# A gated MLP on one core: another order of products seven, three and four, and of the raw products, in the pairs of pass one

## Chip, cores and metric

The kernel runs on one core of a Trainium2 chip. The metric is the device time of one execution in microseconds (us); the median of three runs is compared. In the text TensorE is PE, its weight loads PEld, VectorE DVE, ScalarE ACT, GpSimd POOL, and SP is the engine whose queue issues all the DMAs here.

## What is computed

A gated feed-forward layer on 2048 rows, with inputs and weights in bf16 (x 2048 x 1024, the hidden size is 3584):

```python
g = jnp.einsum("bsd,df->bsf", x, w_gate)
u = jnp.einsum("bsd,df->bsf", x, w_up)
h = _gelu(g) * u
return jnp.einsum("bsf,fd->bsd", h, w_down)
```

## The kernel before

**Passes and units.** The 2048 rows are done in two passes of two blocks of 512 rows. In a pass, the first half makes h: 14 units, each with 256 columns of w_gate and 256 of w_up. The second half multiplies by w_down.

**Products.** A unit treats gate and up as 2 x 2 blocks and multiplies them with seven block products instead of eight. Sums of weight blocks (`s1` to `s4`, made by POOL, and `sa`, a cast by ACT) meet sums of x blocks (`t1` to `t4`, `tb`); these are 128 x 512 matmuls in float32 (fp32r operands). Two of the seven products need no sums: the raw products `raw1` and `raw2` multiply w by x in bf16. A block product is four matmuls for gate and four for up, so eight in all; a half product (`part`) has four.

**Pairs.** In pass one the units 4 to 11 run as four pairs, by `pair0` (L347). Unit a = 4, 6, 8 or 10 is the first of its pair and b = a + 1 the second; n = a + 2 and nn = a + 3 are the units of the next pair, whose raw products the pair computes ahead. Within a pair, the product s1 x t1 of both units is done with half products (`r1` to `r4` and halves of `s1` against `T1` to `T4`, `TB`), whose result for unit b, and that of unit a, is also written to DRAM (`pd`) for use in pass two.

**Banks.** The eight PSUM banks are four pairs of two, called F, C, K and E in a pair; index 0 is gate, 1 is up. A matmul without a fresh start adds to what stands in the bank. So between two products in one bank, other engines copy out (`snap`, ACT), add to it in place (`add`, DVE) or read it (`gelu` on ACT, then `times` on DVE, which multiplies gelu of gate by up into h and reads up from the bank).

**Side work.** The sums of w_down that the second half needs are also made within the pairs, by `keep(j, n, ps)` in three steps: each step is a cast of a w_down piece into a PSUM bank (ACT, L517) and a subtraction (DVE, L518). The three steps use the banks ps[0], ps[1], ps[0], and step two and three subtract the result of the step before. A pair does this for `ja` at its beginning in K, for `jm` (pairs 4 and 6 only, from MID) in its middle in F, and for `jb` at its end in C. `hooks("made", j)` stores such a result, `hooks("fetch", a)` (L416) fetches the next pair's `ja`, `hooks("w", n)` loads the weights of unit n, `hooks("pd", .)` stores to `pd`; all of them are issued by SP in the order of the text.

**What sets the order.** `manual_schedule` keeps the order in which the code issues instructions on PE, DVE, POOL and SP, and within a pass on ACT too. So each engine's queue is the text of `pair0` filtered for that engine, and a product waits where its bank has not been released.

**The PE order of a pair before**, in block products with the bank that they go to:

```
F s2·t2 | E half | C s2·t2 (b) | E half | F s3·t3 | E s4·tb | K r2 half | F sa·t4 |
K r3 half | E r1 half | C s3·t3 (b) | E r4 half | K half |
F raw1 (n) | E raw2 (n) | K s4·tb (b) | C sa·t4 (b) | E raw1 (nn) | K raw2 (nn)
```

These are 124 matmuls, 92 in float32 and 32 in bf16. At the beginning of the next pair its own first half product in E is copied out (`p1`, L377) before the second half product adds to the same bank (L382); the copies stand in ACT's queue behind the gelu of the last raw product of the pair before, one cast of `keep(ja, 0, K)` and the two `u2` copies.

Of the kernel before, what the change touches and what calls it, by code (L numbers as in the profile page):

```python
# [10 lines left out]
def kernel(  # L11
# [32 lines left out]
    ADD, SUB, MUL = ALU.add, ALU.subtract, ALU.mult  # L44
# [17 lines left out]
    JS = {4: (0, 2), 6: (3, 5), 8: (6, 7), 10: (8, 9)}  # L62
    MID = {4: 1, 6: 4}
# [45 lines left out]
    def dve(out, a, b, op):  # L109
        nc.vector.tensor_tensor(out=out, in0=a, in1=b, op=op)  # L110
# [14 lines left out]
    def snap(ps, name, at=None):  # L125
        t = slot([P, N], f32, name) if at is None else at
        nc.scalar.copy(out=t, in_=ps)  # L127
        return t
# [71 lines left out]
    def gelu(src):  # L200
        g = slot([P, N], f32, "g")
        nc.scalar.activation(g, src, ACT.Gelu_apprx_tanh)  # L202
        return g
# [3 lines left out]
    def times(fb, c, g, u):  # L207
        if (fb, c) not in away:
            at = h(fb // NJ, fb % NJ, c)
        else:  # L210
            at = away[fb, c] = away[fb, c]()
        dve(at, g, u, MUL)
# [14 lines left out]
    def add(ps, other):  # L227
        g = new(dve, ps[0], other[0], ADD, "sum", dtype=f32)
        dve(ps[1], ps[1], other[1], ADD)
        return g, ps[1]  # L230
# [85 lines left out]
    def part(ps, lhs, rhs, start, stop=True):  # L316
        for i in range(2):
            for k in range(H):
                matmul(ps[i], lhs[i][:, k, :], rhs[k], start and k == 0, stop and k == H - 1)

    def full(ps, lhs, rhs, start=False):
        for i in range(2):
            product(ps[i], lhs[i], rhs, start)

    def raw1(e, w):
        full(e, [w[:, i, :KH, :P] for i in range(2)], [xT[0][:, k] for k in range(KH)], True)

    def raw2(c, w):
        full(c, [w[:, i, KH:, :P] for i in range(2)], [xT[0][:, KH + k] for k in range(KH)], True)

    def hadd(ps, other, fb, c):
        g, up = add(ps, other)
        g = gelu(g)
        times(fb, c, g, up)
# [8 lines left out]
    def squared(e, p5, fb):  # L343
        dve(e[1], e[1], p5[1], SUB)
        times(fb, 0, gelu(e[0]), e[1])

    def pair0(a, roles, S, t, js, hooks):  # L347
        F, C, K, E = roles
        b, n, nn = a + 1, a + 2, a + 3
        sa, sb = S[a], S[b]  # L350
        q = {}
        t1 = t["t1"]
        A, B = [[flat(xT[1][:, 2 * m : 2 * m + 2]) for m in (2 * n, 2 * n + 1)] for n in range(2)]

        sa.make(*[x for x in ("s1", "s2", "s3") if x not in sa])
        sb.make(*[x for x in ("s1", "s2") if x not in sb])
        form = small_sums((sa, sb), q)
        form("r1"), form("r2")
        if "s4" not in sa:
            sa.make("s4")  # L360
        form("r3")
        sb.make("s3")
        form("r4")
        sb.make("s4")

        def keep(j, n, ps):
            if j is not None:
                keep_part(j, n, ps[n % 2])

        ja, jb = js  # L370
        jm = MID.get(a)
        hooks("w", n)
        keep(ja, 0, K)
        full(F, sa["s2"], t["t2"])
        u2a = [snap(F[i], "u2") for i in range(2)]
        part(E, [x[:, :H] for x in sa["s1"]], t1[:H], True, False)
        p1 = [snap(E[i], "p1", A[i]) for i in range(2)]  # L377
        full(C, sb["s2"], t["t2"])
        keep(ja, 1, K)
        keep(ja, 2, K)  # L380
        hooks("made", ja)
        part(E, [x[:, H:] for x in sa["s1"]], t1[H:], False)  # L382
        p5a = [snap(E[i], "p5") for i in range(2)]
        u2b = [snap(C[i], "u2") for i in range(2)]
        full(F, sa["s3"], t["t3"])
        g, up = add(F, p5a)
        into(K, p1)
        full(E, sa["s4"], t["tb"])
        g = gelu(g)
        times(2 * a + 1, 1, g, up)  # L390
        part(K, q["r2"], T2, False)
        u2r = [snap(K[i], "u2", B[i]) for i in range(2)]
        full(F, sa["sa"], t["t4"])
        hadd(E, u2a, 2 * a, 1)
        part(K, q["r3"], T3, False)
        squared(F, p5a, 2 * a + 1)
        keep(jm, 0, F)
        part(E, q["r1"], T1, True)
        sb.make("sa")
        hooks("w", nn)  # L400
        p5r = [snap(E[i], "p5", A[i]) for i in range(2)]
        full(C, sb["s3"], t["t3"])
        for i in range(2):
            dve(A[i], K[i], p5r[i], ADD)
        keep(jm, 1, F)
        keep(jm, 2, F)
        part(E, q["r4"], TB, False)
        hooks("pd", b)
        part(K, [x[:, H:] for x in sb["s1"]], T4, False)
        hooks("home", b)  # L410
        for i in range(2):
            dve(B[i], E[i], u2r[i], ADD)
        hooks("pd", a)
        if jm is not None:
            hooks("made", jm)
        hooks("fetch", a)  # L416
        p5b = [snap(K[i], "p5") for i in range(2)]
        raw1(F, W(n))
        g, up = add(C, p5b)
        p1n = [snap(F[i], "p1") for i in range(2)]  # L420
        raw2(E, W(n))
        S[n], S[nn] = sums_s(W(n), pool), sums_s(W(nn), pool)
        g = gelu(g)
        times(2 * b + 1, 1, g, up)
        full(K, sb["s4"], t["tb"])
        hadd(E, p1n, 2 * n, 0)
        S[n].make("sa")
        full(C, sb["sa"], t["t4"])
        hadd(K, u2b, 2 * b, 1)
        raw1(E, W(nn))  # L430
        squared(C, p5b, 2 * b + 1)
        keep(jb, 0, C)
        p1nn = [snap(E[i], "p1") for i in range(2)]
        keep(jb, 1, C)
        keep(jb, 2, C)
        raw2(K, W(nn))
        S[n].make("s1", "s2")
        if nn <= LAST:
            S[nn].make("s1", "s2")
        hadd(K, p1nn, 2 * nn, 0)  # L440
        hooks("made", jb)
        return F, E, K, C

    def pair1(a, roles, S, t, hooks):
        F, C, K, E = roles
# [50 lines left out]
    wraw, made = {}, {}  # L496
# [119 lines left out]
    sa = {}  # L616
# [188 lines left out]
    def W(u):  # L805
        if u not in ws:
            ws[u] = load_w(u)
        return ws[u]
# [37 lines left out]
    for ip in range(NPASS):  # L846
        with tc.manual_schedule(engines={ENG.Activation}):
# [6 lines left out]
            for u in range(1 if ip == 0 else 0, NU):  # L854
                if upgraded(u):
                    if u % 2:
                        continue
                    if u == FIRST:
                        S = {u: s, u + 1: sums_s(W(u + 1), pool)}
                    if (ip, u) == (0, FIRST):  # L860
                        fetch_wd(MID.values())
                        for n in range(4):
                            for c in range(2):
                                away[NH + n, c] = lambda n=n, c=c: staged(n, c)
                        away[NH + 4, 0] = lambda: hx

                    def hooks(what, n):
                        if what == "w":
                            W(n)
                            if ip == 0 and n - 3 in JS:  # L870
                                fetch_wd(JS[n - 3][1:])
                            if ip and n <= LAST:
                                fetch_p5(n)
                        if what == "home" and n == LAST:
                            bring_home()
                        if what == "pd":
                            k = 0 if n % 2 else KH
                            nc.sync.dma_start(
                                out=pd[:, n - FIRST].rearrange("p i n -> p (i n)"),
                                in_=flat(xT[1][:, k : k + KH]),  # L880
                            )
                        if what == "made":
                            store_made(n)
                        if what == "fetch":
                            fetch_wd(JS[n + 2][:1] if n + 2 in JS else [10, 12, 13])

                    roles = F, C, K, E
                    if ip == 0:
                        F, C, K, E = pair0(u, roles, S, t, JS[u], hooks)
                    else:  # L890
                        F, C, K, E = pair1(u, roles, S, t, hooks)
                    if u + 1 == LAST:
                        s = make_s(None, pool, S[u + 2])
                        nxt["s"] = S[u + 3]
                    continue
# [19 lines left out]
                def keep(part, ps):  # L915
                    if js:
                        keep_part(js[0], part, ps[part // 2])
                    if ip == 0 and u in (2, 3):
                        for n in ((0, 1), (), (2,))[part]:
                            lo_part(u - 2, n, ps)  # L920
# [92 lines left out]
```

## Time and profile before

| what | value |
|---|---|
| median of three runs | 536.85 us (536.62 to 536.99) |
| the profiled execution, its own time | 536.99 us |
| its span, first to last instruction | 535.2 us |
| PE busy | 529.3 us |
| DVE, ACT, POOL busy | 364.9, 279.8, 261.4 us |
| granted TensorE clock | 1.000 |
| pairs of pass one begin at | 65.65, 93.28, 121.15, 149.03 us |
| unit 12 begins at | 176.90 us |

The span is the time between the first and the last instruction of the program; 1.8 us of the execution's own time lie around it. A line of the timeline gives the start of a group of equal instructions, the time from its first start to its last end, the engine, the source line, the operation with its tiles (out<-in) and shapes, the count, and in brackets the idle time before it with what ended it. Matmuls overlap: one is shown with about 0.39 us, though the next begins some 0.22 us after it, so the steps from start to start are what counts on PE. The first float32 matmul behind bf16 ones is recorded about 0.19 us early and that much longer.

### The profile page before, as it was taken

The numbers are of one execution on the slowest core, as the hardware profiler recorded it, in microseconds if no ns is written. First come the engines' busy times: TensorE is split into PE (matmuls) and PEld (weight loads), VectorE is DVE, ScalarE is ACT, GpSimd is POOL, SyncE is SP. The second block draws the span as 40 slices with busy tenths as digits, with TensorE's granted clock in tenths as the row PEclk, the third lists the DMA queues.
The fourth block names the chain that finished last, engine by engine and source line by source line (L and its number), as shares of the span: only waits on it lengthen the run. The fifth ranks groups of instructions, "written<-read, shape, count | busy, mean of one in ns | idle before, by whom it ended". The sixth has DMA issues, their size and how long they took to land.

```text
span 535.2 us, 7481 instructions
## 1 busy us (share of the span) xinstructions
PE 529.3 (99%) x2372; PEld 377.4 (71%) x2393; DVE 364.9 (68%) x568; ACT 279.8 (52%) x503; POOL 261.4 (49%) x247
## 2 busy tenths in 40 slices
PE   8999999999999999999999999999999999999997
PEld 4568686868677764688886767768667685488886
DVE  2988768787777889459695545576585749675830
ACT  2557686868586731015636555656666650105351
POOL 1179977969799610000008949693979610000000
PEclk9999999999999999999999999999999999999999
DMA  9796318685758899989987343445471149555571
GB/s 246 159 246 173 82 60 294 198 295 198 235 197 288 293 347 391 274 208 224 280 242 196 80 139 99 119 118 157 120 197 54 26 129 391 208 177 168 169 244 50
DMA packets 115527, 103.91 MB, mean 194 GB/s; under 512 B 21792, under 2 KB 97696, under 8 KB 115360
## 3 DMA queue, kind: packets, MB, share of 16 engines
q1 hardware_dynamic: 115488, 103.44, 63.9%
q8 instruction: 19, 0.31, 0.2%
q14 instruction: 20, 0.16, 0.1%
HBM read 78.64 MB, written 19.40 MB: 183 GB/s over the span
## 4 chain that ended last, share of the span: by engine, by line
PE 98%; DMA 1%; issue 0%; SPq 0%; ACT 0%
PE bank L134 98%; DMA xn<-in_x_dram 1%; SPq L705 0%; PE bank L712 0%; ACT st L677 0%
## 5 line engine op out<-in xcount | busy, mean ns | idle before, releaser
L113 POOL TENSOR_TENSOR s<-w 128x512 fp32r<-128x512 bf16 x102 | 119.8, 1195 | 152.1 <-PE bank L134 113.3
L134 PE MATMUL bank<-t,s 128*128 128x512 f32 x552 | 131.6, 392 | 0.0
L134 PEld LDWEIGHTS bank<-t,s 128*128 128x128 f32 x552 | 103.6, 188 | 22.3
L134 PE MATMUL bank<-xT,w 128*128 128x512 bf16 (+1 forms) x489 | 107.8, 376 | 1.0
L134 PEld LDWEIGHTS <-w 128*128 128x128 bf16 x504 | 47.8, 98 | 58.2 <-issue 4.4
L202 ACT ACTIVATE g<-sum 128x512 f32<-128x512 f32 x81 | 51.5, 636 | 64.6 <-DVE sum L110 64.0
L127 ACT COPY p<-bank 128x512 f32<-128x512 f32 x102 | 58.1, 590 | 50.5 <-PE bank L134 50.4
L110 DVE TENSOR_TENSOR sum<-bank,p 128x512 f32<-128x512 f32 x54 | 37.1, 687 | 39.4 <-PE bank L134 38.8
L110 DVE TENSOR_TENSOR hT<-g,bank 128x512 bf16<-128x512 f32 x72 | 49.1, 687 | 17.1 <-ACT g L202 11.3
L113 POOL TENSOR_TENSOR s<-w,s 128x512 fp32r<-128x512 bf16 x50 | 58.1, 1181 | 0.3
L113 POOL TENSOR_TENSOR s<-s,w 128x512 fp32r<-128x512 f32 x50 | 57.6, 1172 | 0.4
L122 ACT CAST tb<-raw 128x512 fp32r<-128x512 bf16 x28 | 17.5, 628 | 72.8 <-PE bank L134 31.0
L134 PE MATMUL bank<-t,sa 128*128 128x512 f32 x216 | 55.0, 397 | 0.0
L134 PE MATMUL bank<-tb,s 128*128 128x512 f32 x216 | 54.3, 393 | 0.0
L110 DVE TENSOR_TENSOR bank<-bank,p 128x512 f32<-128x512 f32 x70 | 48.5, 696 | 7.0 <-PE bank L134 6.8
L134 PE MATMUL bank<-q 128*128 128x512 f32 x208 | 51.7, 389 | 0.0
L134 PEld LDWEIGHTS bank<-t,sa 128*128 128x128 f32 x216 | 40.6, 188 | 9.1
L134 PEld LDWEIGHTS bank<-tb,s 128*128 128x128 f32 x216 | 40.5, 188 | 8.9 <-issue 0.2
L134 PEld LDWEIGHTS bank<-q 128*128 128x128 f32 x208 | 39.0, 188 | 8.1
L127 ACT COPY u<-bank 128x512 f32<-128x512 f32 x56 | 32.2, 594 | 15.1 <-PE bank L134 15.1
L110 DVE TENSOR_TENSOR q<-raw 128x512 fp32r<-128x512 bf16 x28 | 19.2, 687 | 19.2 <-DMA raw<-in_w_down_dram 16.9
L134 PE MATMUL bank<-raw,hT 128*128 128x512 bf16 x140 | 31.2, 379 | 0.2
(80 smaller groups left out, 635.2 us busy)
## 6 DMA issues: line engine op xcount, KB each, us to landing
raw<-in_w_down_dram SPq DMA_DIRECT2D x72, 256.0 KB, 5.3
w<-in_w_gate_dram SPq DMA_DIRECT2D x27, 512.0 KB, 4.3
w<-in_w_up_dram SPq DMA_DIRECT2D x27, 512.0 KB, 5.7
q<-td SPq DMA_DIRECT2D x52, 256.0 KB, 4.4
td<-m SPq DMA_DIRECT2D x12, 768.0 KB, 5.0
w<-td SPq DMA_DIRECT2D x6, 1024.0 KB, 9.6
pd<-xT SPq DMA_DIRECT2D x8, 512.0 KB, 5.9
out_dram<-st SPq DMA_DIRECT2D x32, 128.0 KB, 1.7
```

Source lines behind the costliest of these rows:

```text
L110: nc.vector.tensor_tensor(out=out, in0=a, in1=b, op=op)
L113: nc.gpsimd.tensor_tensor(out=out, in0=a, in1=b, op=op)
L122: nc.scalar.copy(out=t, in_=src)
L127: nc.scalar.copy(out=t, in_=ps)
L134: nc.tensor.matmul(ps, lhsT=lhs, rhs=rhs, start=start, stop=stop, skip_group_check=True)
L202: nc.scalar.activation(g, src, ACT.Gelu_apprx_tanh)
```

## The change

The change is in `pair0`, and in the hook that fetches `jb`. PE's order of a pair becomes:

```
F s2·t2 | E half | C s2·t2 (b) | E half | F s3·t3 | E s4·tb | K r2 half | F sa·t4 |
E r1 half | K r3 half | E r4 half | K half |
C s3·t3 (b) | K s4·tb (b) | C sa·t4 (b) |
F raw1 (n) | E raw2 (n) | C raw1 (nn) | K raw2 (nn)
```

The matmuls are the same in number and kind. `r1` goes before `r3`, the product s3 of unit b behind the half products, s4 and sa of unit b ahead of the raw products, which become one run of 32 bf16 matmuls. The `keep` of the middle moves to the product sa of unit b, in bank E, and exists in all four pairs: where MID has no entry (a = 8, 10), it takes over `jb`, and the `keep` at the end is left out. In pairs 4 and 6 the `keep` at the end stays, in E instead of C, behind the `times` of unit n. The copy of K[1] to `u2r` goes behind a gelu, the casts `sb.make("sa")` and the load of the weights of unit nn behind `gelu(F[0])`, and the fetch of the next `ja` behind the store of `jm`. The new hook fetches `jb` for pairs 8 and 10 at their beginning.

```diff
         ja, jb = js
         jm = MID.get(a)
+        if jm is None:
+            jm, jb = jb, None
         hooks("w", n)
...
         part(K, q["r2"], T2, False)
-        u2r = [snap(K[i], "u2", B[i]) for i in range(2)]
+        u2r = [snap(K[0], "u2", B[0])]
         full(F, sa["sa"], t["t4"])
-        hadd(E, u2a, 2 * a, 1)
+        g, up = add(E, u2a)
+        g = gelu(g)
+        u2r.append(snap(K[1], "u2", B[1]))
+        times(2 * a, 1, g, up)
+        dve(F[1], F[1], p5a[1], SUB)
+        part(E, q["r1"], T1, True)
+        p5r = [snap(E[i], "p5", A[i]) for i in range(2)]
         part(K, q["r3"], T3, False)
-        squared(F, p5a, 2 * a + 1)
-        keep(jm, 0, F)
-        part(E, q["r1"], T1, True)
+        for i in range(2):
+            dve(A[i], K[i], p5r[i], ADD)
+        times(2 * a + 1, 0, gelu(F[0]), F[1])
         sb.make("sa")
         hooks("w", nn)
-        p5r = [snap(E[i], "p5", A[i]) for i in range(2)]
-        full(C, sb["s3"], t["t3"])
-        for i in range(2):
-            dve(A[i], K[i], p5r[i], ADD)
-        keep(jm, 1, F)
-        keep(jm, 2, F)
         part(E, q["r4"], TB, False)
...
-        if jm is not None:
-            hooks("made", jm)
+        full(C, sb["s3"], t["t3"])
+        p5b = [snap(K[i], "p5") for i in range(2)]
+        full(K, sb["s4"], t["tb"])
+        g, up = add(C, p5b)
+        g = gelu(g)
+        times(2 * b + 1, 1, g, up)
+        full(C, sb["sa"], t["t4"])
+        keep(jm, 0, E)
+        keep(jm, 1, E)
+        dve(C[1], C[1], p5b[1], SUB)
+        keep(jm, 2, E)
+        hooks("made", jm)
         hooks("fetch", a)
-        p5b = [snap(K[i], "p5") for i in range(2)]
         raw1(F, W(n))
-        g, up = add(C, p5b)
+        g = gelu(C[0])
         p1n = [snap(F[i], "p1") for i in range(2)]
+        g2, up2 = add(K, u2b)
+        times(2 * b + 1, 0, g, C[1])
+        times(2 * b, 1, gelu(g2), up2)
         raw2(E, W(n))
         S[n], S[nn] = sums_s(W(n), pool), sums_s(W(nn), pool)
-        g = gelu(g)
-        times(2 * b + 1, 1, g, up)
-        full(K, sb["s4"], t["tb"])
-        hadd(E, p1n, 2 * n, 0)
         S[n].make("sa")
-        full(C, sb["sa"], t["t4"])
-        hadd(K, u2b, 2 * b, 1)
-        raw1(E, W(nn))
-        squared(C, p5b, 2 * b + 1)
-        keep(jb, 0, C)
-        p1nn = [snap(E[i], "p1") for i in range(2)]
-        keep(jb, 1, C)
-        keep(jb, 2, C)
+        g, up = add(E, p1n)
+        raw1(C, W(nn))
+        times(2 * n, 0, gelu(g), up)
+        keep(jb, 0, E)
+        p1nn = [snap(C[i], "p1") for i in range(2)]
+        keep(jb, 1, E)
+        keep(jb, 2, E)
         raw2(K, W(nn))
...
         hadd(K, p1nn, 2 * nn, 0)
-        hooks("made", jb)
-        return F, E, K, C
+        if jb is not None:
+            hooks("made", jb)
+        return F, C, K, E
...
-                            if ip == 0 and n - 3 in JS:
-                                fetch_wd(JS[n - 3][1:])
+                            for m in (n - 2, n - 3):
+                                if ip == 0 and m in JS and (m == n - 3) == (m in MID):
+                                    fetch_wd(JS[m][1:])
```

## Prediction

> **What bounds the kernel now.** I read the page first: the busy times and the chain of waits.
>
> ```profile
> span 535.2 us, 7481 instructions
> PE 529.3 (99%) x2372; PEld 377.4 (71%) x2393; DVE 364.9 (68%) x568; ACT 279.8 (52%) x503; POOL 261.4 (49%) x247
> ...
> PE 98%; DMA 1%; issue 0%; SPq 0%; ACT 0%
> ```
>
> PE is the bound through the whole span, and the list of waits has no entry for PE inside the four pairs. A change of order that keeps all matmuls can therefore win only what PE loses between its matmuls, and can lose without limit, by making PE wait. What it can win shows in the timeline of PE in the pair that begins at 93.28:
>
> ```profile
> 109.84 1.07 PE L134 MATMUL bank<-forms,s 128*128 128x512 f32 x4
> 110.75 3.63 PE L134 MATMUL bank<-xT,w 128*128 128x512 bf16 x15
> 114.03 2.19 PE L134 MATMUL bank<-tb,s 128*128 128x512 f32 x8
> 116.06 0.39 PE L134 MATMUL bank<-t,sa 128*128 128x512 f32 x1
> ...
> 69.28 3.11 PE L134 MATMUL bank<-t,s 128*128 128x512 f32 x13
> 124.99 3.14 PE L134 MATMUL bank<-t,s 128*128 128x512 f32 x13
> ```
>
> A float32 step is (3.11 - 0.39) / 12 = 0.227 us (row at 69.28), a bf16 step (3.63 - 0.38) / 15 = 0.217 (the run has 16, one record is missing). From 109.84 to 116.06 stand 4 + 8 float32 and 16 bf16 matmuls: 12 x 0.227 + 16 x 0.217 = 6.19, against 6.22 measured. With the first bf16 step, which is some 0.01 longer, a change to bf16 and back costs about 0.04 us.
>
> The last row shows the other thing to know. These 13 matmuls, in the pair that begins at 121.15, take 0.03 us longer than the same count in the first pair. The 23rd matmul of the pair (about 126.36) is the first that adds to E[1] again, and it needs the copy of E[1] to `p1`. Before it stand ACT and DVE:
>
> ```profile
> 119.81 0.59 ACT L127 COPY p<-bank 128x512 f32<-128x512 f32 x1 [0.28 <-PE bank L134]
> 120.30 1.11 ACT L517 CAST bank<-raw 128x512 f32<-128x512 bf16 x2
> 123.04 0.63 ACT L202 ACTIVATE g<-sum 128x512 f32<-128x512 f32 x1 [1.63 <-DVE sum L110]
> 123.58 0.58 ACT L517 CAST bank<-raw 128x512 f32<-128x512 bf16 x1
> 124.09 1.07 ACT L127 COPY u<-bank 128x512 f32<-128x512 f32 x2
> 125.05 1.09 ACT L127 COPY xT<-bank 128x512 f32<-128x512 f32 x2
> ```
>
> ```profile
> 120.92 1.49 DVE L110 TENSOR_TENSOR m<-bank,m 128x512 fp32r<-128x512 f32 x2 [0.39 <-ACT bank L517]
> 122.33 0.68 DVE L110 TENSOR_TENSOR sum<-bank,p 128x512 f32<-128x512 f32 x1
> ```
>
> The last copy (the second of the row at 125.05) ends at 126.14, 0.22 before that matmul. The three pairs with this 0.22 lose 0.03 us there, the first pair, with its copy over a microsecond earlier, nothing. So I read 0.22 us as what PE needs from the end of a release to the matmul, and the margin as used up. Everything in front hangs together: ACT is without a break from the gelu at 123.04, which waited for the sum at 122.33, which stood in DVE's queue behind the three subtractions of the `keep` at the end.
>
> **The change part by part.** Rates from these rows: ACT starts a copy every 0.48, behind a cast or gelu 0.52 to 0.54; DVE every 0.60, or 0.80 where it uses the result just before. An engine starts 0.04 after its releaser's end; a bank's last matmul counts to its shown end (start + 0.39). I put the new order on the clock of the pair at 93.28, up to `K r2` at 102.59 unchanged.
>
> *One run of 32 bf16 matmuls*: one round trip less in each of four pairs, 4 x 0.04 = -0.16. Bounds: 0, and -0.45, all that a pair loses beyond its steps: 27.87 - 92 x 0.227 - 32 x 0.216 = 0.1, four times.
>
> [...]
>
> *r1 ahead of r3.* Rows of this pair: DVE's sum of E[0] starts 103.46, the gelu follows at 104.18 and ends 104.81 (no longer behind K[1]'s copy, which moves to 104.70), `times` 104.85 to 105.54. E[1] of r1 is due at 105.31 + 2 x 0.227 = 105.76, and 105.54 + 0.22 = 105.76: no margin, where there was 0.9 (r3's length). Copies of E to p5r: 105.97 and 106.45 to 107.03; r4 needs E[0] at 107.13 and E[1] at 107.58: 0.3 left. The sums into A: 106.87 and 107.48 to 108.17; the second half product in K is due at 108.03 and 108.49: 0.25 and 0.10 left.
>
> *Products s3, s4, sa of b, and the middle `keep`.* They run 108.94, 110.75, 112.57, the raw products from 114.38 (F), 116.11 (E), 117.84 (C), 119.56 (K). The add to C and its `times` end at 112.44, C[1] is due at 113.48: covered. sa ends (last shown end) at 114.55; DVE then does C[1] minus p5b at 114.58 and the third subtraction of the `keep` at 115.19 to 115.88; with 0.22 that is 116.10, raw2 in E[0] is due at 116.12. No margin again. For these two places the cost lies between 0 and 0.1 in each of four pairs; between ends that far apart I take the 0.03 of the row at 124.99 for three of the eight places, +0.1.
>
> *The end of a pair with the `keep` there (4 and 6).* This is where the time goes. DVE has six operations in a row behind sa (third subtraction 115.19, K[0] 115.79, K[1] 116.40, two `times` 117.00 and 117.60), so the sum of E[0] for unit n starts only at 118.21, although its product ends at 117.2. The gelu follows at 118.93, and ACT, in order, has behind it: cast of step one 119.47, the copies of raw1 (nn) 119.98 and 120.46, the cast of step two 120.94 to 121.53 (before: 120.30 was its start). Then DVE: step two 121.57, step three 122.37, the sum of K[0] 122.97 to 123.65, and the gelu of K starts 123.69, against 123.04 before, while the next pair begins 0.04 earlier: 0.69 late. The cast and the four copies behind it keep their steps. Step three, which ends at 123.06, also lets go of E[0] late: due at 123.14, possible at 123.28, 0.14, part of the 0.69. So the pairs of units 6 and 8, which follow pairs 4 and 6, each lose 0.69 at the matmul that was due without margin: +1.38. If the 0.22 is margin and not latency, it is 0.47 each, +0.94.
>
> [...]
>
> *The end of the pairs without it (8 and 10)*: the three subtractions are gone, the sum of K[0] is free as soon as its product ends, about two microseconds earlier. The pair of unit 10 loses its 0.03: -0.03. No more can be won, PE does not wait there.
>
> *Moved DMAs.* The load of unit nn is issued behind the sa casts, at 108.6 instead of 107.13. Its landings released POOL 4.1 and 5.9 after the issue; later by 1.5 they come at 115.0, raw1 (nn) is due at 117.84. POOL's chain behind it ends 1.5 later: r4 of the next pair at 131.4 for a matmul due at 135.0, s4 of b at 133.1, due 138.6. Cover in all cases: two microseconds and more. The fetch of the next `ja` moves from 112.50 behind the store of `jm`, to about 116.6 and 117.5; w_down pieces here take 4.3 to 7.3 to land (median 5.9), so 122.5, and the cast that needs it is ready at 124.2. Covered up to 7.3; behind pairs 8 and 10 the cast could go earlier, but isn't needed earlier. SP's queue behind the fetch has nothing that is due.
>
> *Sum*: -0.16 + 0.1 + 1.38 - 0.03 = +1.3 on the profiled execution's 536.99 (535.2 span and 1.8 around it), 538.3. That execution is 0.14 above the median, so on the median's scale **538.2 us**.
>
> **The rivals.**
> *The cover holds.* ACT or DVE catch up (the sum of E[0] only has to come 0.7 earlier), or the margin at the 23rd matmul is larger than its 0.03 suggests. For it: the waits name no PE wait at all in these pairs. Against: 0.03 in just the three pairs whose copy comes 0.22 ahead. Then 536.85 - 0.16 - 0.03 = 536.7, no difference that can be measured.
> *The next `ja` comes too late.* For it: its fetch is 4.1 later, and SP's issues there take up to 1.2. Against: landings of 4.3 to 7.3. It decides from a landing of over 7.6 us behind an issue at 116.6; a landing of 8.5 gives 0.9 more at two pairs, and 540.0.
> *It does not do what it says*: the switches cost nothing or come back elsewhere. That takes 0.16 off the gain and is inside the ranges.
> *Faster beyond a measurement's reach* would need over 1.07 us, twice the 0.45 that the pairs have to give.
>
> **How the numbers follow.** A measurement of this kernel tells 0.2%, 1.07 us, from no change: same is 535.8 to 537.9. Forecast, two waits: 0.60, own range 537.6 (536.85 - 0.19 + 0.94, no other cost) to 538.7 (536.85 - 0.19 + 1.38 and 0.1 at six of the eight tight places), with some 0.52 of its chance above 537.9. The cover holds: 0.27. `ja` late, or another of the tight places much dearer: 0.09. Faster: 0.04. Slower is 0.52 + 0.09 = 0.61, same 0.08 + 0.27 = 0.35, faster 0.04. The range takes the rival of no change in and leaves the late `ja` mostly out: 536.6 to 539.2.
>
> **What would show it.** Right: PE's float32 rows behind the first two long bf16 runs have a gap of 0.5 to 0.7 us at the first half product's second part (E), with ACT's copy in front of it and the gelu of K over two microseconds behind the pair's beginning; the third pair's row has none; bf16 runs of 32, and no other PE wait over 0.1. Wrong: four equal pairs (cover holds, or one of the two tight places inside the pair decides), an ACT cast with a DMA as releaser at the beginning of a pair (`ja`), or PE waiting behind r1 or in raw2.

## The result, and the profile after

| kernel | median | range | runs |
|---|---|---|---|
| before | 536.86 us | 536.56 to 536.99 | 6 |
| changed | 538.81 us | 538.19 to 539.36 | 6 |

The ratio is 1.0036, with a 95% interval of 1.0023 to 1.0049: the changed kernel is slower, by some 1.9 us. The profiled execution of the changed kernel took 539.16 us, with a span of 537.4. In the line numbers of the changed kernel the casts of `keep` are at L527; the other lines that the text names in ACT's and DVE's rows are as before.

From the page of the changed kernel, the busy times and the first line of the chain that ended last:

```profile
span 537.4 us, 7492 instructions
PE 531.0 (99%) x2372; PEld 377.1 (70%) x2393; DVE 365.3 (68%) x568; ACT 280.1 (52%) x503; POOL 262.6 (49%) x247
...
PE 72%; DMA 2%; DVE 1%; ACT 0%; issue 0%; SPq 0%; ACTq 0%
```

PE's share of busy time has stayed at 99%, and yet the chain is no longer all PE: it runs through a DMA and DVE somewhere. The busy time alone would have hidden that.

Where the time went shows in the stretches between the beginnings of the pairs. The columns are from and to, length, and busy time (instructions) of PE, PEld, DVE, ACT and POOL, then the granted clock and the DMA's share. Before:

```profile
65.65:93.28 27.63, 27.58 (x125) 20.09 (x124) 20.11 (x32) 20.90 (x40) 20.21 (x21) 1.00 0.48 172
93.28:121.15 27.87, 27.82 (x125) 20.24 (x125) 22.37 (x36) 21.72 (x42) 23.49 (x25) 1.00 0.70 237
121.15:149.03 27.88, 27.81 (x126) 20.23 (x125) 20.72 (x33) 20.18 (x39) 24.30 (x26) 1.00 0.63 207
149.03:176.90 27.87, 27.80 (x126) 20.24 (x125) 20.70 (x33) 20.19 (x39) 24.49 (x24) 1.00 0.79 270
```

After:

```profile
65.11:92.69 27.58, 27.51 (x124) 20.16 (x124) 19.97 (x31) 20.25 (x39) 18.82 (x19) 1.00 0.50 171
92.69:121.52 28.83, 28.41 (x125) 20.02 (x125) 22.37 (x35) 21.75 (x42) 23.00 (x24) 1.00 0.67 227
121.52:150.01 28.49, 28.22 (x126) 20.02 (x125) 22.18 (x35) 21.01 (x40) 24.52 (x26) 1.00 0.71 234
150.01:177.81 27.80, 27.73 (x126) 20.31 (x125) 20.76 (x33) 20.26 (x38) 26.07 (x26) 1.00 0.69 238
```

The four pairs differ by -0.05, +0.96, +0.61 and -0.07, together +1.45 us. The two that follow pairs 4 and 6 lose, the other two win a little. The span grew by 2.2; the rest falls outside of the pairs, as shown further down.

**The loss behind a pair's beginning.** PE's timeline in the pair that begins at 121.52, and PE's weight loads in the pair that begins at 92.69:

```profile
121.52 4.98 PE L134 MATMUL bank<-t,s 128*128 128x512 f32 x20
126.71 3.08 PE L134 MATMUL bank<-t,s 128*128 128x512 f32 x12 [0.20 <-ACT xT L127]
```

```profile
97.87 0.30 PEld L134 LDWEIGHTS bank<-t,s 128*128 128x128 f32 x2 [0.64 <-ACT xT L127]
98.36 0.76 PEld L134 LDWEIGHTS bank<-t,s 128*128 128x128 f32 x4 [0.19 <-ACT xT L127]
```

The wait is where the prediction put it, at the second half product in E, for the copies to `p1`. Matmul by matmul the step is 0.37 to 0.38 too long at the first waiting one and 0.11 too long at the next. Both belong to one wait: the waiting matmul is recorded 0.50 long in place of 0.39, so its start is shown some 0.11 early. With 0.03 ahead of it and 0.03 behind it, each of the two pairs loses 0.55 in these steps; the 0.03 ahead stands at the first half product in E, whose bank the third step of the `keep` lets go. The work in front of it, ACT's and DVE's timelines at the end of pair 6 and the beginning of the next:

```profile
124.05 0.63 ACT L202 ACTIVATE g<-sum 128x512 f32<-128x512 f32 x1 [1.63 <-DVE sum L110]
124.59 0.58 ACT L527 CAST bank<-raw 128x512 f32<-128x512 bf16 x1
125.10 1.07 ACT L127 COPY u<-bank 128x512 f32<-128x512 f32 x2
126.05 1.09 ACT L127 COPY xT<-bank 128x512 f32<-128x512 f32 x2
```

```profile
118.58 0.68 DVE L110 TENSOR_TENSOR sum<-bank,p 128x512 f32<-128x512 f32 x1
...
121.93 1.49 DVE L110 TENSOR_TENSOR m<-bank,m 128x512 fp32r<-128x512 f32 x2 [0.67 <-ACT bank L527]
123.33 0.68 DVE L110 TENSOR_TENSOR sum<-bank,p 128x512 f32<-128x512 f32 x1
```

The gelu of K starts 2.53 us after its pair's beginning (124.05 - 121.52), before it was 1.89. It is 0.64 late, and the chain in front is the predicted one: the sum of E[0] late, the three steps of `keep`, the sum of K[0], the gelu, a cast, four copies.

**A second loss, in pair 6 alone.** The 12 matmuls of `r1`, `r3` and `r4` in PE's timeline, for pair 6 and pair 8, and the `times` that `r1` waits for in DVE's:

```profile
105.27 3.33 PE L134 MATMUL bank<-forms,r 128*128 128x512 f32 x12
...
134.16 2.93 PE L134 MATMUL bank<-forms,r 128*128 128x512 f32 x12
```

```profile
105.28 0.69 DVE L110 TENSOR_TENSOR hT<-g,bank 128x512 bf16<-128x512 f32 x1 [0.48 <-ACT g L202]
...
133.78 0.69 DVE L110 TENSOR_TENSOR hT<-g,bank 128x512 bf16<-128x512 f32 x1 [0.15 <-ACT g L202]
```

Pair 6 loses 0.40 us here against pair 8. The gelu in front ended at 104.91 and 133.75, so the same instruction followed its releaser in 0.36 us in one pair and in 0.03 in the other.

**A third, at the end of pass one.** DVE's timeline there, the waits of PE's weight loads from 268 to 276 (total, times, longest), and PE's timeline:

```profile
264.53 0.69 DVE L110 TENSOR_TENSOR s<-w 128x512 fp32r<-128x512 bf16 x1 [5.14 <-DMA w<-in_w_gate_dram]
266.32 0.69 DVE L110 TENSOR_TENSOR s<-w 128x512 fp32r<-128x512 bf16 x1 [1.10 <-DMA w<-in_w_up_dram]
...
270.54 1.88 DVE L110 TENSOR_TENSOR st<-bank,m 128x512 bf16<-128x512 f32 x3
272.34 0.68 DVE L110 TENSOR_TENSOR st<-bank,p 128x512 bf16<-128x512 f32 x1
```

```profile
PEld bank L134 <- DVE st L110: 1.2, 3, 0.4
```

```profile
271.32 5.88 PE L134 MATMUL bank<-q,sa 128*128 128x512 f32 x20
```

The same two engines before:

```profile
269.65 0.68 DVE L110 TENSOR_TENSOR st<-bank,p 128x512 bf16<-128x512 f32 x1
270.35 6.96 PE L134 MATMUL bank<-q,sa 128*128 128x512 f32 x30
```

DVE makes the first weight sums of pass two (`make_s(ws[0])`, for the weights that are loaded at step 50) in its queue ahead of four stores `st`, and those release the banks that PE's first `sa` product there writes. The weights landed late, the sums and so the stores came late, and PE lost 1.36 us in five steps from 271.3 to 273.4. Before, the fourth store ended at 270.33 and that product began at 270.35, without a gap; here the product began at 271.32, behind the first store, and the fourth ended only at 273.01. With 1.45 in the pairs that would be 2.81; the span's difference is 2.2, since this execution was 0.54 ahead when its first pair began (65.11 against 65.65) and won 0.1 between the pairs and the boundary.

### The profile page after: what moved, and what is told of

Same layout as the page of the kernel before. It is cut to its first block, busy times and chain, and to the rows that moved or that the text cites. A ratio compares the mean times of both kernels' runs of the same rounds, so it can differ in the third digit from the quotient of the medians.

```text
span 537.4 us, 7492 instructions
## 1 busy us (share of the span) xinstructions
PE 531.0 (99%) x2372; PEld 377.1 (70%) x2393; DVE 365.3 (68%) x568; ACT 280.1 (52%) x503; POOL 262.6 (49%) x247
## 4 chain that ended last, share of the span: by engine, by line
PE 72%; DMA 2%; DVE 1%; ACT 0%; issue 0%; SPq 0%; ACTq 0%
PE bank L134 72%; DMA w<-in_w_up_dram 2%; DVE s L110 1%; DVE st L110 0%; SPq L728 0%; ACT u L127 0%; ACT st L687 0%; SPq L144 0%; ACT xT L127 0%; SPq L574 0%; ACT bank L527 0%; ACTq L127 0%; ACT g L202 0%; DVE bank L110 0%
## 5 line engine op out<-in xcount | busy, mean ns | idle before, releaser
L113 POOL TENSOR_TENSOR s<-w 128x512 fp32r<-128x512 bf16 x102 | 121.2, 1210 | 153.2 <-PE bank L134 124.5
```

Of the source, the lines that this page charges most:

```text
L113: nc.gpsimd.tensor_tensor(out=out, in0=a, in1=b, op=op)
```

## The experiments

Theory: the time goes into three waits of PE, and the largest is the chain at the end of pairs 4 and 6, from DVE's row of operations through the `keep` to the copies of `p1`. Rivals: a place-bound loss of another kind in the first two pairs; the boundary between the passes. The first four rows ran on one chip, the other four on a second; ratios are to the kernel before on the same chip, with the 95% interval, so between the two groups only ratios are compared.

| kernel | median | ratio | lengths of the pairs, us | gap at the boundary |
|---|---|---|---|---|
| before_again | 537.09 | 1.0000 (0.9991 to 1.0009) | 27.63, 27.87, 27.87, 27.87 | none |
| after_again | 538.70 | 1.0032 (1.0019 to 1.0045) | 27.64, 28.83, 28.50, 27.84 | 0.33 |
| add_first | 537.23 | 1.0003 (0.9995 to 1.0012) | 27.62, 28.03, 27.96, 27.83 | none |
| load_46 | 538.27 | 1.0023 (1.0014 to 1.0032) | 27.62, 28.82, 28.50, 27.83 | none |
| pool_jb | 536.99 | 0.9997 (0.9988 to 1.0006) | 27.62, 27.81, 27.82, 27.82 | 0.16 |
| pool_jb_46 | 536.88 | 0.9997 (0.9988 to 1.0006) | 27.64, 27.82, 27.82, 27.82 | none |
| shift_12 | 538.12 | 1.0016 (1.0008 to 1.0025) | 27.62, 28.49, 28.48, 27.82 | none |
| tail_in_all | 539.77 | 1.0048 (1.0035 to 1.0062) | 27.64, 28.79, 28.48, 28.49 | none |

**The two kernels once more**: before_again and after_again, without an edit.

> The kernel before once more, for its pass boundary and its scatter. Theory B with a margin: no PE gap at the boundary in this profile, times 536.6 to 537.0. If late landings hit the kernel before as well, one of its times lies a microsecond higher or its profile has a boundary gap.

> The changed kernel once more. Theory A (ACT's queue at the end of pairs 4 and 6 delays the p1 copies): the pairs that begin with units 6 and 8 again have a PE gap of about 0.55 us each at the second half product in E; the pair of unit 10 has none. Theory B (the rest of the loss, 1.36 us at 271 to 273 us of the profile, is the w_gate/w_up load of unit 0 for pass two landing late behind full DMA engines, and comes and goes): the gap at the pass boundary differs from the first profile and the times scatter by a microsecond again. If the boundary gap is a fixed part of the change, it is 1.4 us again and the median near 538.8.

The difference is there again, 1.6 us. The lengths of the two longer pairs come back to 0.01 us, the gap at the boundary does not: 0.33 in place of 1.36.

**add_first** moves one operation, the last `times` of unit b, behind the sum of E[0] for unit n:

```diff
-        times(2 * b, 1, gelu(g2), up2)
+        g2 = gelu(g2)
...
         g, up = add(E, p1n)
+        times(2 * b, 1, g2, up2)
         raw1(C, W(nn))
```

> At the end of a pair DVE adds p1n to E (unit n) before it does the times of K instead of behind it; nothing else. Theory A: the gelu of unit n comes 0.6 to 0.9 us earlier, the casts and copies behind it on ACT too, and the PE gaps of 0.55 us in the pairs of units 6 and 8 go to 0 to 0.1: 0.9 to 1.1 us faster than the changed kernel, near 537.7. Rival (the late gelu of K comes from the moved fetch of ja or from the earlier product order, not from that queue): gaps and time as in the changed kernel.

0.0029 less in the ratio than after_again, some 1.5 us, for an edit of order on DVE alone. ACT's gelu of K at the beginning of the second of the two pairs, which begins at 121.46:

```profile
123.46 0.63 ACT L202 ACTIVATE g<-sum 128x512 f32<-128x512 f32 x1 [1.63 <-DVE sum L110]
```

The gelu of K starts 2.06 and 2.00 us behind the pairs' beginnings in place of 2.53, and the two gaps behind them shrink from 0.55 to 0.10 and 0.05: the chain is shown to be the cause. More came back than expected, since the gap behind `r1` in pair 6 (0.06 left) and that at the boundary were gone as well.

**load_46** loads the first weights of pass two at step 46:

```diff
-            if step == 50:
+            if step == 46:
```

> The changed kernel with the weight load of units 0 and 1 of pass two issued at step 46 of the second half instead of 50. Theory B: the boundary gap (1.36 us in the first profile) is gone in this profile, the times scatter by 0.5 us or less and lie near the low end of the changed kernel's, 538.0 to 538.3; the gaps in the pairs stay. If the boundary gap is not the load's landing: no difference to the changed kernel, 538.8.

The gap at the boundary goes, the pairs stay as they were: the losses are independent. The time is 0.4 us less, about the gap of 0.33, though the two intervals overlap.

**pool_jb** takes `jb` out of the end of pairs 4 and 6 altogether: POOL makes those sums, and `jb` is fetched at the beginning of all four pairs (that part of the edit is not shown).

```diff
-        keep(jb, 0, E)
...
-        keep(jb, 1, E)
-        keep(jb, 2, E)
...
+        if jb is not None:
+            ra, rb = wraw[jb]
+            made[jb] = three(f32r)
+            m = [made[jb][:, i] for i in range(3)]
+            pool(m[0], ra[:, N:], ra[:, :N], SUB)
+            pool(m[1], rb[:, N:], m[0], SUB)
+            pool(m[2], rb[:, :N], m[1], SUB)
...
```

> The changed kernel, but the sums jb of pairs 4 and 6 are made by POOL, with three subtractions straight from the w_down pieces, in place of the keep at the end of these pairs; jb is fetched at the beginning of all four pairs. Theory (the keep at the end delays DVE's and ACT's chain in front of the first half product's second part): without it the gaps of about 0.5 us there go, as in add_first; -1.1 us against the changed kernel, down to -1.5 if the gap behind r1 in pair 6 goes as well; so 537.2 to 537.6, and at best 0.2 below the kernel before. Rival (POOL becomes late): POOL has about 2 to 3 us more to do at the end of two pairs; if the sums r or s4 of the next pair come late for it, PE waits at those matmuls instead, and the time stays at 538.5 or goes above.

The stretches of pool_jb, first and second pair:

```profile
66.12:93.74 27.62, 27.55 (x125) 20.16 (x124) 19.77 (x31) 19.49 (x37) 22.33 (x22) 1.00 0.52 177
93.74:121.55 27.81, 27.74 (x125) 20.32 (x125) 20.75 (x33) 20.25 (x38) 27.22 (x28) 1.00 0.72 237
```

The waits of PE inside the pairs are gone; the list of waits has no entry for PE there. The second pair has 1.6 us less of DVE (20.75 against 22.37) and 4.2 more of POOL, which is busy nearly all of it and still not late. So the order of products of the change costs nothing in itself: without the `keep` at the end, the pairs are 0.05 shorter than before (27.82 against 27.87). The sum of four, 111.07 against 111.25, is what the change had to give. It can't be seen in the time: no difference.

**pool_jb_46** adds the load at step 46, twice.

> As pool_jb, and the load of the first weights of pass two four steps earlier. Theory: the landing of that load has no part in the end of pass one any more, so this is pool_jb without the gap at the pass boundary where it had one: 0 to -0.4 us against pool_jb, 536.7 to 537.2. Rival (the earlier load only moves contention elsewhere): no better than pool_jb.

> pool_jb_46 once more, beside before_load_46: by the lengths of the pairs (27.82 against 27.87 in three of them) it is 0.15 us shorter than the kernel before, 0.03%, which five rounds can hardly tell from nothing: 536.7 to 537.0.

The first time 536.88 beside 537.15 for the kernel before, the second, on a third chip, 537.18 beside 537.01 (ratio 1.0004, 0.9996 to 1.0013). The best version that the experiments point to is equal to the kernel before; none beats it by anything that five rounds can tell.

**shift_12** adds twelve memsets of 128 x 1 on DVE, some 60 us ahead of the place in question.

```diff
+    pad = xpool.tile([P, 1], f32, name="pad")
...
+                    if (ip, u) == (0, 2):
+                        for _ in range(12):
+                            nc.vector.memset(pad, 0.0)
```

> The changed kernel with twelve tiny DVE instructions (a memset of 128 x 1) added at unit 2, long before the pairs. Theory (the lag of 0.36 us at the times of r1 in pair 6 falls on every 62nd or so DVE instruction, and happens to hit this one): the lag moves to another instruction, PE's gap behind r1 in pair 6 shrinks from 0.4 to 0.1 us or less, and the time falls by about 0.3 us, to 538.2 to 538.4; the two gaps behind the pairs' beginnings stay, unless the lag lands in front of them. Rival (the lag belongs to this place, by its wait for the gelu): the gap of 0.4 stays as it is, 538.7.

DVE's and PE's timelines of shift_12 at `r1` of pair 6:

```profile
105.59 0.69 DVE L110 TENSOR_TENSOR hT<-g,bank 128x512 bf16<-128x512 f32 x1 [0.15 <-ACT g L202]
...
105.94 2.94 PE L134 MATMUL bank<-forms,r 128*128 128x512 f32 x12
```

With nothing changed near it, the `times` follows its gelu at once, and PE's 12 matmuls take 2.94 in place of 3.33: the lag does not belong to the place. The pair is 28.49 long, as the one behind it. The time fell somewhat more than the expected 0.3, as this profile also has no gap at the boundary; against load_46, which has none either, the ratio is 0.0007 less, 0.4 us, though the two intervals overlap.

**tail_in_all** repeats the `keep` at the end in pairs 8 and 10 too, for the sums of `jm` once more:

```diff
+        jt = jm if jb is None else jb
-        keep(jb, 0, E)
+        keep(jt, 0, E)
...
```

The other two steps change in the same way.

> The changed kernel, with the keep at the end in all four pairs: in pairs 8 and 10 it repeats the casts and subtractions of jm. Theory: the pair of unit 10 gets the same gap of about 0.5 us in front of the first half product's second part that the pairs of units 6 and 8 have, +0.5 us; behind pair 10 stands unit 12, which has other work at its beginning, so little there: 539.0 to 539.3. Rival (the gaps belong to something else that the first two pairs have): the pair of unit 10 keeps its length of 27.8 us, no change.

Third and fourth pair of tail_in_all:

```profile
122.19:150.67 28.48, 28.21 (x126) 20.00 (x125) 22.37 (x35) 21.68 (x42) 24.48 (x26) 1.00 0.71 236
150.67:179.16 28.49, 28.22 (x126) 20.02 (x125) 22.37 (x35) 21.67 (x42) 26.02 (x26) 1.00 0.68 234
```

The pair of unit 10 becomes 28.49 long, the same to 0.01 as that of unit 8, with the same wait for ACT's copy (0.20 in its timeline). The rival of something peculiar to the first two pairs falls. Where the expectation was short: unit 12 has a wait of this kind too, 0.64 us in four steps behind 183.4, and with the 0.65 of the pair and no gap at the boundary (0.33 in after_again) this makes 1.0, for the 0.9 (0.0016 of 537) between the ratios of tail_in_all and after_again.

**The boundary from the other side**, on a third chip: the kernel before with its load two steps later, and four steps earlier.

```diff
-            if step == 50:
+            if step == 52:
```

> The kernel before, with the load of the first weights of pass two two steps later (52 in place of 50), some 3.9 us. Theory (DVE makes the first sums of pass two ahead of the four stores st that PE's first sa product of the boundary needs, and those sums wait for this load; the kernel before has only some 0.4 us of margin there): the sums and the stores move back by 3 to 4 us and PE gets a gap at the boundary, at about 271: +3 to +4 us, 540 to 541. Rival (the gap of the changed kernel at the boundary has another cause, such as the later end of its pairs): no gap, 537.

> The kernel before with that load four steps earlier. Theory: the kernel before has no gap at the boundary in the profiles, so nothing to win: 536.8 to 537.1, beside the kernel before on the same chip.

DVE's and PE's timelines of before_load_52:

```profile
266.85 0.69 DVE L110 TENSOR_TENSOR s<-w 128x512 fp32r<-128x512 bf16 x1 [8.15 <-DMA w<-in_w_gate_dram]
...
273.67 11.70 PE L134 MATMUL bank<-q,sa 128*128 128x512 f32 x41 [3.05 <-issue]
```

Three stretches of before_load_52, with the columns of the tables above (the granted clock stands third from the end):

```profile
274.60:275.60 1.00, 1.00 (x3) 0.48 (x3) 1.00 (x3) 0.00 (x0) 0.00 (x0) 0.50 1.03 371
275.60:276.60 1.00, 1.00 (x4) 0.82 (x4) 1.00 (x3) 0.00 (x0) 0.00 (x0) 0.50 1.04 387
277.70:279.00 1.30, 1.30 (x7) 1.08 (x6) 1.30 (x4) 0.20 (x1) 0.00 (x0) 1.00 1.10 381
```

542.84 us, ratio 1.0107 (1.0093 to 1.0120), so +5.8 where 3 to 4 were expected. The mechanism is shown: the late weights alone make the gap in a kernel whose pairs are untouched. The size was wrong because I counted only the first wait (3.2). Behind it PE first goes at DVE's pace, one store each 0.6 us, which adds 0.32, 0.37, 0.37 and 0.36. Then the stores no longer hold it, but the granted clock is 0.50 (from 274.19 to 277.60), and the steps of 0.43 in place of 0.227 add 0.20, 0.20, 0.20 and 0.16. Together this is 5.4. In its four executions the clock over the whole span was 0.994 to 0.997, in those of the kernel before on that chip 0.999 to 1.000. The other one, before_load_46, 537.24 (1.0001, 0.9992 to 1.0010), has nothing to win, as expected: the kernel before has just enough margin.

## Why the prediction was nearly right

**The bound and the place**: right. The loss is PE waiting at the second half product in E, in the pairs of units 6 and 8 and in no other, for copies behind a gelu that starts over two microseconds after the pair's beginning; add_first, pool_jb and tail_in_all show the chain in three ways. One sign that the prediction named for being wrong came as well, PE waiting behind r1, but in pair 6 alone.

**The ends of pairs 4 and 6, +1.38**: the mechanism right, each term 0.14 too large, 0.55 in place of 0.69. The gelu is 0.64 late, not 0.69, which is 0.05 of the 0.14; 0.03 is what these pairs had lost before already. The rest is the step "I read 0.22 us as what PE needs from the end of a release to the matmul, and the margin as used up". It is neither all latency nor all margin. The first and the second copy of `p1` end 4.496 and 4.982 behind the pair's beginning before, 5.133 and 5.620 after; a weight load starts at 4.547, 5.033, 5.184 and 5.671: 0.051 later each time. Where PE stood still, the matmul followed the second of these loads, at 5.671, after 0.114 (5.785, when its extra recorded time is taken off). So a release cost PE 0.165 us here, and 0.055 of the 0.22 was margin. The release of E[0] by the third step, priced at 0.14 within the 0.69, cost the 0.03 ahead of the wait. The 0.03 us that the prediction built on had another origin than a matmul at its limit: the load for E[1] came 0.06 late there (5.033, undisturbed 4.974), which cost the matmul 0.005 and left 0.03 in the steps behind it.

**`r1` ahead of `r3`, and raw2 in E, +0.1 for eight places without margin**: half right. At raw2 no step is 0.02 too long. At `r1` pairs 6 and 8 lose 0.03 to 0.06 where nothing else happens (after_again, shift_12), so the estimate of 0.03 held; "no margin" was the finding, but I priced it by a quiet execution. A lag of 0.36 us in DVE fell on this `times`, which had 0.9 of cover before, and went straight to PE: 0.37 to 0.40 in pair 6, in both profiles of the changed kernel and in those of load_46 and tail_in_all.

**One run of 32 bf16 matmuls, -0.16**: the size of one switch was right, the sum less sure. In the profile of the changed kernel the first pair, which has no loss at `p1`, is 0.04 shorter (27.587 against 27.627), and the pair of unit 10 is 0.07 shorter, 0.04 and the 0.03 of `p1`. In the repeat the first pair is 27.64, and in pool_jb 27.62: there 0.03 to 0.05 are lost at the second half product in K, which the prediction gave 0.10 and 0.25 to spare. pool_jb's four pairs are together 0.18 shorter than before, but some 0.09 of that is the loss at `p1`.

**Pair of unit 10, -0.03, and the moved DMAs**: right. In the pair that begins at 92.69 the load of unit nn was issued 16.3 behind the beginning and the fetch of `ja` 24.0, where the prediction has 15.3 and 23.3 (108.6 and 116.6, from 93.28); the two waits of PE in this pair, 0.55 and 0.40, lie ahead of both. No cast waited for a DMA at the beginning of a pair; one did in unit 12, 0.45 us at 179.21.

**What was missing**: the boundary. The prediction says nothing of what lies behind the pairs, as if 1.3 us of delay just moved it. It does not: SP's load for pass two and DVE's sums meet PE there with little margin, and the loss is 1.36 and 0.33 us in the two profiles of the changed kernel. That the delay of the pairs makes the weights late is not shown: tail_in_all comes to the boundary latest of all and has no gap.

**The sum**: +1.3 predicted, +1.45 in the four pairs of the profile. That they agree is in part an accident: two terms 0.14 too large and one place 0.40 where some 0.03 was allowed, nearly cancel. The measured median of 538.81 (538.70 again) is 0.5 to 0.6 above 538.2; the boundary, which has no term in the sum, cost 1.36 and 0.33 in the two profiles. Of the rivals, "the cover holds" was right only for pairs 8 and 10, the late `ja` didn't come, and the switches gave what they promised in one profile of two.

## What to carry to other kernels

A `keep`, or any block of side work, that is moved behind other work of the same engine moves what queues behind it (here the gelu of K, by 0.64 us); follow that queue into the next iteration up to the first matmul that waits, and price the wait there. Where a move takes a place's margin to zero, the price is not the mean lateness but the hiccups that the margin had swallowed: 0.03 to 0.06 us was the quiet loss behind `r1`, 0.37 to 0.40 the one with DVE's lag. And look once at the end of a pass: where DMA, side engine and PE meet with half a microsecond to spare (0.53 in the kernel before: the fourth store ended at 270.33, the fourth matmul of that product began at 271.03, less 0.165 for the release), a late transfer goes straight to PE, in the changed kernel with 1.36 and 0.33 us.

## What the runs showed of the hardware

**In these runs some operations of DVE started 0.32 to 0.45 us behind their release, at places that lie 128 records apart or a multiple of it.** If all of DVE's records in a trace are counted, its waits and semaphore instructions among them, the late `times` at `r1` is record 192, in both profiles of the changed kernel and in those of load_46 and tail_in_all. Lags of this size behind a release stand also at records 448 (before_again at 246.00, 0.44; add_first at 233.94, 0.45), 576 (tail_in_all at 316.00, 0.45; before_load_46 at 324.23, 0.32) and 704 (before_load_46 at 397.42, 0.45). With twelve more instructions ahead of it, shift_12 has another operation in place 192, at 99.48, and the `times` starts at once. Not every such place lags: in the kernel before, DVE still worked on the operation in front of record 192 (105.51), and the one at 99.48 in shift_12, which had waited 1.65 us for ACT, followed its release in 0.02. Late starts outside of these places exist too, such as two sums into A in the changed kernel (0.74 at 107.31, 0.40 at 135.81), which wait for the product `r3` as well.

What the engine waits for there is not shown. Near the lag lies one block of 8,192 bytes that moves on queue 14, of the kind "instruction", 0.67 to 0.69 us behind the start of the late `times` (105.95 in the changed kernel, 106.44 in after_again, 106.66 in tail_in_all). The kernel before moves one at 106.21 too, 0.70 behind the start of its record 192, which did not lag. The queue moves 26 such blocks in the trace of the changed kernel, and DVE's 909 records have only seven of these places, so whether the block has to do with the lag stays open.

**A release cost PE 0.165 us where it stood still, in two pairs of the changed kernel.** It is 0.051 from the shown end of ACT's copy to the start of the weight load, and 0.114 from there to the matmul. The second part is what shows as 0.108 to 0.114 at the second matmul behind each wait in the pairs, since the record of the waiting matmul begins with its weight load and is that much longer. The load of the second matmul is early again: it starts 0.23 ahead of it (97.98 and 98.21), as where nothing waits (0.22).

**In before_load_52 the granted clock fell behind a stop of PE.** PE stood for 3.05 us, and 0.5 us after it began again the clock was 0.50 for 3.4 us. That the stop brought it down is not shown. Behind the waits of the changed kernel at the boundary, none longer than 0.4, it stayed at 1.00.

**Why the weights landed late at the boundary stays open.** SP's timeline of the changed kernel and of the kernel before shows where the changed kernel's queue is first held much longer:

```profile
258.71 3.95 SPq L144 DMA_DIRECT2D w<-in_w_gate_dram  x1
```

```profile
257.92 1.88 SPq L144 DMA_DIRECT2D w<-in_w_gate_dram  x1
```

The third of the four issues took 3.95 us in place of 1.88, and the first weight sum, which waits for the first landing, started 7.07 us behind that load's issue in place of 5.15; in after_again it is 6.02, in add_first 5.62. Why the queue takes longer there was not tried.
